# Pooled attention feeding an MLP: values of batch 0 pooled in halves, first h tiles by token halves, values of batch 1 loaded between the quarters of w2

## The chip, the cores and the metric

The kernel runs on one core of one Trainium2 chip. The metric is device time in microseconds; the number given for a kernel is the median of its runs. A profile is one separate execution with every instruction and DMA packet recorded.

A core has a matrix engine (PE, with a weight-load side PEld), VectorE (DVE), ScalarE (ACT), GpSimd (POOL) and SyncE (SP). PE writes PSUM, 8 banks of 512 fp32 columns on 128 partitions. DMAs are issued from SP, ACT or POOL; POOL's are the ones that convert types on the way.

## The reference

```python
# q, k, v: (8, 8, 576, 64) fp32; pool 8 -> 72 pooled rows per head
k_p = k.reshape(B, H, 72, 8, D).mean(axis=3)
v_p = v.reshape(B, H, 72, 8, D).mean(axis=3)
attn = softmax(q @ k_p^T / sqrt(D))
x = (attn @ v_p).transpose(0, 2, 1, 3).reshape(4608, 512)
h = x @ w_in            # 512 x 2048
g = h - tanh(h)
out = g @ w_out         # 2048 x 512
```

## The kernel before, in words

**Tiling.** A batch has 576 tokens. The first 512 of each batch make a token group (groups 0 to 7); the last 64 of all eight batches make group 8. For a group, h is computed transposed: 16 tiles of 128 features by 512 tokens, each from 4 matmuls over the 512 inputs (`w1b` stationary, `xT` moving), then Tanh on ACT and a subtraction on DVE into `Gt`. The second product uses `w2b`. Groups 1 to 8 do it with seven half-size products of sums of blocks of `Gt` and of w2 (L713 to L721): `w2s` holds the sums of w2 (`sum0` to `sum3`, `negated`), `w_sum` overwrites b12 in `w2b`, and DVE makes `P`, `Q`, `Dg` from `Gt`. Group 0 uses the plain product, `mlp_o(0, tb, qd, gts)` (L610): 4 token blocks by 4 quarters of w2 in the order `W2_ORDER = (0, 8, 4, 12)`.

**Order of the work.** The program has no scheduler (`manual_schedule`): each engine runs its instructions in the order in which the code issues them, so the code order is the order in each engine's queue, with semaphore waits between engines. A DMA issued from a queue whose semaphore is still held by an older DMA waits for that one; POOL has eight such semaphores and uses them in turn.

**Start (L783 to L1073).** Batch 0 and batch 1 are done by a special route so that PE has work while weights and inputs are still coming in. k of batch 0 is pooled on DVE (`pool_k`), turned on PE against an identity (`k_turn`), q is cast on ACT and turned on PE (`q_pe_transpose`), scores and exponentials follow (`scores_wide`). k and v rows lie as pairs of heads: 4 pairs of 128 rows, and 4 times 16 left-over rows in a fifth slot (`NM`). v of batch 0 is loaded by POOL as bf16 (`v_bf`) and pooled on PE: `v_pe_pool` accumulates 8 matmuls; `v_main` and `v_left` multiply with a mask into `VB`. `av_pair(p, half, b0)` computes attention times v for token blocks 2p and 2p+1 and four heads, normalises on DVE and writes `x0`; `x0_turn` turns it on PE and ACT copies it into `xT[0]`. `h_open` runs the first two of the four matmuls of h tiles 3, 0, 1, 2, 4. Between these steps stand `warm_pe(n)` calls (L777): matmuls on zeros that nothing reads. 30 are issued in all, 10 of them after q's last transposes.

Then tiles 0 to 4 get their other two matmuls and Tanh and subtraction (L975), tiles 5 to 15 follow (L980), and k, q, v of batch 1 and `mlp_o` of group 0 are interleaved (L1011 to L1069): `pool_k(1, nc.gpsimd, last=nc.vector)`, `k_transpose(1)`, `q_pe_transpose(1)`, `pool_v1` on DVE, `scores_wide(1)`, `av(1, blk)`, `turn1(blk)`.

**Loads that matter here.** POOL issues, in this order: v of batch 0 (L828), four quarters of w1 (`load_w1`), w2 rows 0 to 3 of 16 (`load_w2(0, 4)`), q of batch 1 (L838, L839), `load_w2(8, 4)`; after `pool_k(1)`, `load_w2(4, 4)` and `load_w2(12, 4)`. SP issues k of batch 1 when w1's second quarter has landed (L848), then v of batch 1 in two halves (L972, L973), and k of batch 2 when the third w2 load, `w2_dmas[2]`, has landed (L1043). ACT issues the left-over rows of v of batch 1 (L913); DVE pools them at L974.

**Groups 1 to 8 (L1075 to L1142).** `h_pair` makes two h tiles at a time, DVE subtracts (L646) and sums (L654); then the products, with scores and attention of the next batch among them. In group 1, DVE also runs `sum2(4)` (L1086) and the `w_sum` of b12 (L1088).

Of the kernel before, what the change touches and what calls it, by code (L numbers as in the profile page):

```python
# [20 lines left out]
R = 4  # L21
# [22 lines left out]
def kernel(  # L44
# [252 lines left out]
                out=vps[b][:, :, :], in0=r[:, :, 0, :], in1=r[:, :, 1, :], op=ALU.add  # L297
            )

    def pool_v1(ta, tb):  # L300
        r = v_raw[1].rearrange("p t (j d) -> p t j d", d=D)
        for n in (4, 2, 1):
            nc.vector.tensor_tensor(
                out=r[:, ta:tb, 0:n, :],
                in0=r[:, ta:tb, 0:n, :],
                in1=r[:, ta:tb, n : 2 * n, :],
                op=ALU.add,
            )
        if ta == NM:
            return v_left(VB[1], r[:, NM, 0:1, :], nc.vector)  # L310
        return v_main(VB[1], r[:, :, 0:1, :], nc.vector, ta, tb)

    vps = {}

# [6 lines left out]
    def v_main(vb, vs, eng, t0, t1):  # L321
        n = t1 - t0
        return eng.tensor_tensor(
            out=vb[:, 2 * t0 : 2 * t1, 0:D].rearrange("p (t s) d -> p t s d", s=2),
            in0=vs[:, t0:t1, :, :].to_broadcast([128, n, 2, D]),
            in1=mask[:, 2 * t0 : 2 * t1, :]
            .rearrange("p (t s) o -> p t s o", s=2)
            .to_broadcast([128, n, 2, D]),
            op=ALU.mult,
        )  # L330

    def v_left(vb, vs, eng):
        return eng.tensor_tensor(
            out=vb[:, 2 * NM :, 0:D],
            in0=vs.to_broadcast([128, NM, D]),
            in1=mask[:, 2 * NM :, :].to_broadcast([128, NM, D]),
            op=ALU.mult,
        )
# [67 lines left out]
    def scores_wide(b, ts):  # L406
        if b not in E_tiles:
            E_tiles[b] = work.tile([128, H, S], BF16, name="E", tag="E", bufs=1)[:, 0:NT, :]
        E = E_tiles[b]
        for t in ts:  # L410
            ps = ps_any([128, QA], FP32, "s_ps")
            score_mms(b, t, ps[:, :], False)
            nc.scalar.activation(out=E[:, t, 0:QA], in_=ps[:, :], func=ACT.Exp, scale=SCALE)
# [63 lines left out]
                stop=True,  # L477
            )

    def av_mms(b, blk, half, ps):  # L480
        E = E_tiles[b]
        vb = VB[b % 2]
        c0 = blk * 128 if blk < 4 else S - 128
        for n in range(3):
            t = 2 * half + n if n < 2 else NM
            s0 = 2 * t if n < 2 else 2 * NM + 2 * half
            nc.tensor.matmul(  # L487
                ps[:, 2 * n : 2 * n + 2, :].rearrange("p h d -> p (h d)")
                if n < 2
                else ps.rearrange("p (a s) d -> p a s d", s=2)[:, :, 1, :],  # L490
                lhsT=E[:, t, c0 : c0 + 128],
                rhs=vb[:, s0 : s0 + 2, :].rearrange("p h d -> p (h d)")
                if n < 2
                else vb[:, s0 : s0 + 2, :],
                start=(n == 0),
                stop=(n == 2),
                skip_group_check=True,
            )
# [82 lines left out]

    h_tiles = {}

    def mlp_h_mms(g, i, f0, f1, pool=None):
        if f0 == 0:
            h_tiles[i] = ps_h.tile([128, TG]) if pool is None else pool
        for fb in range(f0, f1):
            nc.tensor.matmul(
                h_tiles[i][:, :],
                lhsT=w1b[:, fb, i * 128 : (i + 1) * 128],  # L590
                rhs=xT[g][:, :, fb, :],
                start=(fb == 0),
                stop=(fb == NFB - 1),
            )

    def mlp_h_act(i, gts):
# [180 lines left out]
    def warm_pe(n, cols=512, b0=4):  # L777
        for _ in range(n):
            nc.tensor.matmul(
                bank(b0, [128, cols]), lhsT=zeros[:, 0:128], rhs=zeros[:, 0:cols], start=True, stop=True  # L780
            )
# [43 lines left out]
        )  # L825
    for i in range(2):
        nc.gpsimd.tensor_scalar_mul(VB[i][:, :, D:D1], mask[:, :, :], float(POOL))
    nc.gpsimd.dma_start(out=v_bf[:, 0:NM, :], in_=v_pairs[0, 0:128, :, :])  # L828
    nc.gpsimd.memset(spread[:, :], 0.0)
    nc.gpsimd.tensor_copy(  # L830
        out=spread.rearrange("p (t x) -> p t x", x=32)[:, :, 0:LO],
# [12 lines left out]
    nc.gpsimd.memset(k_raw[1][:, NM, :], 0.0)  # L844
    nc.gpsimd.memset(v_raw[0][:, NM, :], 0.0)
    nc.gpsimd.memset(KB[1][:, :], 0.0)

    after(load_k(1), w1_dmas[1])  # L848

# [50 lines left out]
    pool_k(0, nc.vector, NM, NT)  # L900
    warm_pe(2)
    q_pe_transpose(0, (2, 3), "act")
    warm_pe(2)
    scores_wide(0, (2, 3))
    k_turn_left()
    warm_pe(2)
    v_ps = v_pe_pool(NM, NT, spread)
    scores_wide(0, (NM,))
    v_left(VB[0], v_ps[:, 0, :, :], nc.vector)
    vs = v_pe_pool(0, NM, ident, 4)  # L910
    v_main(VB[0], vs, nc.vector, 0, 2)
    v_main(VB[0], vs, nc.vector, 2, 4)
    load_left(v_pairs, v_raw[1], 1, nc.scalar)  # L913
    gts = []

    def av_pair(p, half, b0):
        ps = PS[:, b0 : b0 + 2, 0 : 4 * D1].rearrange("p k (h d) -> p k h d", d=D1)
        for k in range(2):
            av_mms(0, 2 * p + k, half, ps[:, k, :, :])
        rden = work.tile([128, 2, 4, 1], FP32, name="rden2", tag="rden2")  # L920
        nc.vector.reciprocal(out=rden[:, :, :, :], in_=ps[:, :, :, D:D1])
        nc.vector.tensor_tensor(
            out=x0[:, 2 * p : 2 * p + 2, half, :, :],
            in0=ps[:, :, :, 0:D],
            in1=rden[:, :, :, :].to_broadcast([128, 2, 4, D]),
            op=ALU.mult,
        )
# [17 lines left out]
            in_=ps,  # L945
        )

    def h_open(i, b0):
        mlp_h_mms(0, i, 0, 2, bank(b0, [128, TG]))

    warm_pe(2, b0=3)
    av_pair(0, 0, 2)
    av_pair(1, 0, 5)
    av_pair(0, 1, 0)
    warm_pe(1)
    x0_turn((0, 1), 0, 7, nc.scalar.copy)
    av_pair(1, 1, 2)
    warm_pe(1)
    x0_turn((2, 3), 0, 5, nc.scalar.copy)
    warm_pe(2)  # L960
    h_open(3, 4)
    x0_turn((0, 1), 1, 7, nc.scalar.copy)
    h_open(0, 0)
    h_open(1, 1)
    x0_turn((2,), 1, 5, nc.scalar.copy)
    x0_turn((3,), 1, 6, nc.vector.tensor_copy)
    h_open(2, 2)
    h_open(4, 3)
    ps_any = ps_b1
    ps_h.n = ps_o.n = 0  # L970
    nc.scalar.copy(out=q_bf[:QT, R, :, :], in_=t0[:QT, :, R, :])
    load_main(v_pairs, v_raw[1], 1, 0, 2)  # L972
    load_main(v_pairs, v_raw[1], 1, 2, 4)  # L973
    pool_v1(NM, NT)  # L974
    for i in range(5):  # L975
        mlp_h_mms(0, i, 2, 4)
        mlp_h_act(i, gts)


    for i in range(5, NHID):  # L980
        mlp_h(0, i, gts, bank(i % 5, [128, TG]))
# [26 lines left out]
    def sum3(k0):  # L1008
        return w_sum(w2s[:, 3, :, :], b21, b11, ALU.subtract, k0=k0, k1=k0 + 4)

    pool_k(1, nc.gpsimd, last=nc.vector)  # L1011
    load_w2(4, 4)
    load_w2(12, 4)
    for h in (0, 4):
        nc.vector.tensor_copy(
            out=q_bf[:, 0:R, h : h + 4, :].rearrange("p j h d -> p h j d"),
# [9 lines left out]
    q_pe_transpose(1, (2, 3), "act")  # L1026
    q_pe_tail(1)
    scores_wide(1, (0,))
    pool_v1(2, 4)
    sum1(0)  # L1030
    mlp_o(0, 0, 1, gts)
    scores_wide(1, (1,))
# [4 lines left out]
    sum2(0)  # L1037
    sum0(0)
    sum3(0)
    mlp_o(0, 2, 1, gts)  # L1040
    mlp_o(0, 3, 1, gts)
    ps_a.n = 0
    after(load_k(2), w2_dmas[2])  # L1043
    load_v(2)
    load_q(2)
    av(1, 0, ps_any, True)
    av(1, 1, ps_any, True)
    sum1(4)
    sum0(4)
    mlp_o(0, 0, 2, gts)  # L1050
    turn1(0)
    mlp_o(0, 1, 2, gts)
    turn1(1)
    av(1, 2, ps_any, True)
    av(1, 3, ps_any, True)
    negated(1)
    sum3(4)
    mlp_o(0, 2, 2, gts)
    turn1(2)
    mlp_o(0, 3, 2, gts)  # L1060
    turn1(3)
    av(1, 4, ps_any, True)
    x_pairs.pop((1, 0))
# [1 line left out]
    x_dma_transpose(1, 2)  # L1065
    pool_k(2, nc.gpsimd)
    k_dma_transpose(2)
    for tb in range(4):
        mlp_o(0, tb, 3, gts)  # L1069
    load_k(3)  # L1070
    pool_v(2, nc.gpsimd, (0, 1))
    k_place(2, nc.gpsimd.tensor_copy)
# [2 lines left out]
    for g in range(1, NG):  # L1075
        nb = g + 1 if g + 1 < B else None
        nn = g + 2 if g + 2 < B else None
        for p in range(NP - 1):
            if g == 1 and 2 <= p < 5:
                q_cast_part(2, p - 2)  # L1080
                q_dma_transpose(2, p - 2)
            if nb is not None and g > 1 and p < 3:
                q_cast_part(nb, p)
            h_pair(g, p, ((6, 4, 2, 6, 0, 2, 4) if g == 1 else (0, 2, 4, 6, 0, 2, 4))[p], p % 2)
            if g == 1 and p == 1:
                sum2(4)  # L1086
            if g == 1 and p == 2:
                w_sum(b12, b22, b12, ALU.subtract)  # L1088
            if g == 1 and p == 4:
                store(0, 0, 2, nc.sync)  # L1090
                store(0, 2, 4, nc.sync)
                load_v(3)
                load_q(3)
                v_spread(2, nc.gpsimd)
            if 3 <= p < 6:
                sum_p(2 * p - 6, 2 * p - 4)
            if g > 1 and p == 0:
                if nb is not None:
                    k_dma_transpose(nb)
                store(g - 1, 2, 4, nc.gpsimd)  # L1100
                store(g - 1, 0, 2, nc.gpsimd)
                if nb is not None:
                    k_place(nb, nc.gpsimd.tensor_copy)
            if nb is not None and g > 1 and p < 3:
                q_dma_transpose(nb, p)
            if nb is not None and g > 1 and p == 2:
                v_spread(nb)
                if nn is not None:
                    load_k(nn)
                    load_v(nn)  # L1110
                    load_q(nn)
# [69 lines left out]
```

## Time and profile before

| | us |
|---|---|
| median of 3 runs | 285.9 (285.72 to 285.92) |
| profiled execution, own time | 286.52 |
| profiled execution, span of the core | 284.8 |
| PE busy (share of span) | 275.7 (97%) |
| DVE busy | 222.8 (78%) |
| ACT busy | 154.6 (54%) |
| POOL busy | 113.1 (40%) |
| group 1 h stage begins (L632) | 54.71 |
| group 2 h stage begins (L632, in the chain) | 84.32 |

The span is what the profile's times count from 0; the profiled execution took 1.7 us more than it. Durations are read from the profiled execution, and a change worked out from them is carried to the median. A matmul's recorded duration includes the time in the pipeline: 512 columns show 0.38 us, but they start 0.2155 us apart, and it is the distance that adds up. Idle time of PE is what counts when PE is the busiest engine; idle time of others is harmless unless PE waits for them.

In the timeline, a row is: start, busy time, engine, source line, operation, output<-inputs, shape, count, and in brackets the idle time of the engine before it with what ended it. "SPq", "ACTq" and the POOL rows named DMA_DIRECT2D are issues of DMAs, not their transfer. The trace also has, for each DMA, the times of its 16 completion signals, one from each DMA engine; a DMA has landed with the last of them.

### The profile page before, as it was taken

Reading aid. Unit: us, or ns where it says so; the run is one execution under the profiler, and the core shown is the slowest. Engines: PE = TensorE matmul, PEld = TensorE weight load, DVE = VectorE, ACT = ScalarE, POOL = GpSimd, SP = SyncE. Lnnn points to the kernel's source line nnn. Section 1 sums busy time; section 2 is a strip of 40 time slices with the busy share of each in tenths; the row PEclk is TensorE's granted clock in tenths of the full one; section 3 lists DMA queues with packets and bytes.
Section 4 is the critical chain, followed back from the end, with each engine's and each line's share of the span. In section 5 each row is a group of like instructions: output and inputs, shape, how many; then the busy total and the mean of one; then the engine's idle time right before and its main releaser. Section 6 shows DMA issues by size and latency. Waiting matters only on the chain.

```text
span 284.8 us, 5460 instructions
## 1 busy us (share of the span) xinstructions
PE 275.7 (97%) x2156; PEld 179.8 (63%) x2156; DVE 222.8 (78%) x342; ACT 154.6 (54%) x207; POOL 113.1 (40%) x125
## 2 busy tenths in 40 slices
PE   7799999999999999999999999999999999999994
PEld 2364445644894489548954895479547954884583
DVE  6569889489985998599859985998599839936983
ACT  4637656396528671857186708670868056216610
POOL 8630611991299019901990099009910110010000
PEclk9999999999999999999999999999999999999999
DMA  7999999999947894979789946896640540011014
GB/s 247 226 213 266 272 195 282 253 233 239 286 84 161 245 345 92 155 227 334 133 107 297 348 97 125 286 310 129 114 161 0 76 157 0 2 74 77 0 37 113
DMA packets 66731, 49.82 MB, mean 175 GB/s; under 512 B 42088, under 2 KB 55928, under 8 KB 66706
## 3 DMA queue, kind: packets, MB, share of 16 engines
q1 hardware_dynamic: 56082, 34.92, 48.9%
q0 software_dynamic: 8432, 12.72, 19.0%
q10 hardware_dynamic: 2192, 1.84, 2.2%
q8 instruction: 17, 0.28, 0.4%
q14 instruction: 8, 0.07, 0.1%
HBM read 36.70 MB, written 9.44 MB: 162 GB/s over the span
## 4 chain that ended last, share of the span: by engine, by line
PE 80%; DMA 12%; DVE 4%; POOL 1%; ACT 1%; issue 0%; ACTq 0%; POOLq 0%
PE PS L632 35%; PE PS L689 35%; DMA w2b<-in_moe_w_out_dram 9%; PE PS L616 4%; DMA v_raw<-in_v_dram 3%; PE PS L472 3%; PE PS L446 3%; DVE Gt L646 2%; DVE P L654 1%; PE PS L487 0%; PE PS L398 0%; DVE w2b L672 0%; ACT TS L645 0%; PE PS L566 0%; POOL w2s L839 0%
## 5 line engine op out<-in xcount | busy, mean ns | idle before, releaser
L632 PE MATMUL PS<-xT,w1b 128*128 128x512 bf16 (+1 forms) x504 | 98.0, 355 | 0.0
L646 DVE TENSOR_TENSOR Gt<-PS,TS 128x1024 bf16<-128x1024 f32 x56 | 68.3, 1220 | 35.3 <-ACT TS L645 35.3
L632 PEld LDWEIGHTS <-w1b 128*128 128x128 f16 x576 | 56.4, 98 | 52.8
L645 ACT ACTIVATE TS<-PS 128x1024 f32<-128x1024 f32 x56 | 57.4, 1025 | 29.6 <-PE PS L632 28.1
L733 POOL TENSOR_TENSOR m<-O,m 128x512 f32<-128x512 f32 x6 | 7.6, 1261 | 78.4 <-ACT m L731 78.4
L261 POOL TENSOR_TENSOR k_raw<-k_raw 128x512 f32<-128x512 f32 (+2 forms) x13 | 21.5, 1673 | 26.1 <-DMA k_raw<-in_k_dram 14.2
L689 PE MATMUL PS<-w2s,Dg 128*128 128x256 f16 x256 | 30.2, 272 | 0.0
L467 ACT ACTIVATE E<-PS 72x1024 bf16<-72x1024 f32 (+1 forms) x30 | 26.1, 930 | 4.2 <-PE PS L446 4.1
L689 PEld LDWEIGHTS <-Gt 128*128 128x128 bf16 x256 | 23.5, 98 | 6.8 <-issue 2.3
L689 PEld LDWEIGHTS <-P 128*128 128x128 bf16 x256 | 24.6, 98 | 3.0
L689 PEld LDWEIGHTS <-Dg 128*128 128x128 bf16 x256 | 24.6, 98 | 2.8
L654 DVE TENSOR_TENSOR P<-Gt 128x1024 bf16<-128x1024 bf16 x32 | 21.9, 686 | 0.5
L740 ACT COPY m<-PS 128x512 f32<-128x512 f32 x8 | 4.7, 586 | 29.6 <-PE PS L689 29.6
L664 DVE TENSOR_TENSOR Dg<-Gt 128x1024 bf16<-128x1024 bf16 x32 | 20.4, 681 | 0.0
L705 POOL DMA_DIRECT2D out_dram<-O x14 | 7.7, 553 | 31.6 <-DVE O L743 29.5
L523 DVE TENSOR_TENSOR x_sb<-PS,rden 128x512 bf16<-128x512 f32 x28 | 19.4, 691 | 1.0
L282 POOL TENSOR_TENSOR v_raw<-v_raw 128x512 f32<-128x512 f32 (+1 forms) x12 | 18.2, 1540 | 0.0
L689 PE MATMUL PS<-w2s,Gt 128*128 128x256 f16 x128 | 16.4, 273 | 0.0
L689 PE MATMUL PS<-w2b,P 128*128 128x256 f16 x128 | 16.3, 273 | 0.0
L689 PE MATMUL PS<-w2b,Gt 128*128 128x256 f16 x128 | 16.3, 272 | 0.0
L689 PE MATMUL PS<-w2s,Q 128*128 128x256 f16 x128 | 16.3, 272 | 0.0
L1143 ACT COPY O<-PS 128x512 f32<-128x512 f32 x7 | 4.1, 586 | 21.9 <-PE PS L689 21.9
(123 smaller groups left out, 394.9 us busy)
## 6 DMA issues: line engine op xcount, KB each, us to landing
k_raw<-in_k_dram SPq DMA_DIRECT2D x7, 1024.0 KB, 6.0
out_dram<-O POOLq DMA_DIRECT2D x14, 512.0 KB, 3.8
v_raw<-in_v_dram SPq DMA_DIRECT2D x6, 1024.0 KB, 8.1
q_raw<-in_q_dram SPq DMA_DIRECT2D x6, 1024.0 KB, 10.6
w1b<-in_moe_w_in_dram POOLq DMA_DIRECT2D x4, 512.0 KB, 14.9
w2b<-in_moe_w_out_dram POOLq DMA_DIRECT2D x4, 512.0 KB, 16.6
v_raw<-in_v_dram SPq DMA_DIRECT2D x2, 512.0 KB, 12.1
out_dram<-O SPq DMA_DIRECT2D x2, 512.0 KB, 4.2
```

The costliest lines, as they stand in the source:

```text
L261: eng.tensor_tensor(out=r[:, ta:tb, 0:4, :], in0=r[:, ta:tb, 0:4, :], in1=r[:, ta:tb, 4:8, :], op=ALU.add,)
L282: eng.tensor_tensor(out=r[:, ta:tb, 0:4, :], in0=r[:, ta:tb, 0:4, :], in1=r[:, ta:tb, 4:8, :], op=ALU.add,)
L446: nc.tensor.matmul(dst, lhsT=kv[a * D : (a + 1) * D, m, :], rhs=rhs, start=True, stop=True,)
L467: nc.scalar.activation(out=e, in_=ps, func=ACT.Exp, scale=SCALE)
L523: nc.vector.tensor_tensor(out=x_sb[:, :, :, :], in0=ps[:, :, :, 0:D], in1=rden[:, :, :, :].to_broadcast([128, 2, 4, D]), op=ALU.mult,)
L616: nc.tensor.matmul(o_ps[:, :], lhsT=gts[i][:, tb * 128 : (tb + 1) * 128], rhs=w2b[:, i, :], start=(i == 0), stop=(i == NHID - 1),)
L632: nc.tensor.matmul(dst[:, t0 * 128 : t1 * 128], lhsT=w1b[:, fb, i * 128 : (i + 1) * 128], rhs=x[:, t0:t1, fb, :], start=(fb == 0), stop=(f ...
L645: nc.scalar.activation(out=t2, in_=PS[:, b0 : b0 + 2, :], func=ACT.Tanh)
L646: nc.vector.tensor_sub(out=Gt[:, p, :, :], in0=PS[:, b0 : b0 + 2, :], in1=t2)
L654: nc.vector.tensor_tensor(out=P[:, a:b, :], in0=Gt[:, a:b, 0, :], in1=Gt[:, a:b, 1, :], op=ALU.add)
L664: return nc.vector.tensor_tensor(out=Dg[:, a:b, :, :], in0=Gt[:, a:b, :, 0:HT], in1=Gt[:, a:b, :, HT:TG], op=ALU.subtract,)
L689: nc.tensor.matmul(part(g, bk, tt), lhsT=lhs(k, slice(tt * 128, (tt + 1) * 128)), rhs=rhs[:, k, :], start=(first and k == 0 and (tt == 0 o ...
```

## The change

What it does, part by part:

1. v of batch 0 is loaded by two DMAs of two head pairs each, and pooled on PE in two halves: pairs 0 and 1 ahead of `scores_wide(0, (2, 3))`, pairs 2 and 3 after the left-over scores. The left-over part is pooled ahead of `k_turn_left`.
2. `av_pair(·, 0, ·)` is split: the matmuls of pairs 0 and 1 for both block pairs, then those of the left-over rows, then the normalisation. The h tiles 0 to 3 are built in quarters by `h_part`: two of the four matmuls, for two of the four token blocks, with 256 columns each. Tile 4 is made whole afterwards. PSUM banks are assigned anew. Six of the 30 `warm_pe` matmuls go.
3. The left-over rows of v of batch 1 are pooled on POOL at L914's place instead of on DVE after the h openings.
4. The two main loads of v of batch 1 are issued by POOL: the first between `load_w2(8, 4)` and `load_w2(4, 4)`, the second between `load_w2(4, 4)` and `load_w2(12, 4)`. The two w2 loads are issued before `pool_k(1)` instead of after it. k of batch 2 waits for the second v load instead of `w2_dmas[2]`.
5. `pool_v1(2, 4)` on DVE comes after the sums; `mlp_o` of w2's third quarter for blocks 0 and 1 comes ahead of `av(1, 0)`, and the later `mlp_o` calls move up by two places each.
6. `sum2(4)` and the `w_sum` of b12 move from inside group 1 to ahead of it.

```diff
-    def pool_v1(ta, tb):
+    def pool_v1(ta, tb, eng=nc.vector):
...
+    def mlp_h_mms(g, i, f0, f1, pool=None, t0=0, t1=4):
+                h_tiles[i][:, t0 * 128 : t1 * 128],
+                rhs=xT[g][:, t0:t1, fb, :],
+                start=(fb == 0 and t0 == 0),
...
-    nc.gpsimd.dma_start(out=v_bf[:, 0:NM, :], in_=v_pairs[0, 0:128, :, :])
+    for ta in (0, 2):
+        nc.gpsimd.dma_start(out=v_bf[:, ta : ta + 2, :], in_=v_pairs[0, 0:128, ta : ta + 2, :])
...
+    load_main(v_pairs, v_raw[1], 1, 0, 2, nc.gpsimd)
+    load_w2(4, 4)
...
-    warm_pe(2)
+    vs0 = v_pe_pool(0, 2, ident, 4)
+    v_main(VB[0], vs0, nc.vector, 0, 2)
+    warm_pe(1, b0=3)
     scores_wide(0, (2, 3))
+    v_ps = v_pe_pool(NM, NT, spread)
     k_turn_left()
-    warm_pe(2)
-    v_ps = v_pe_pool(NM, NT, spread)
+    v_left(VB[0], v_ps[:, 0, :, :], nc.vector)
+    warm_pe(1, b0=3)
     scores_wide(0, (NM,))
-    v_left(VB[0], v_ps[:, 0, :, :], nc.vector)
-    vs = v_pe_pool(0, NM, ident, 4)
-    v_main(VB[0], vs, nc.vector, 0, 2)
-    v_main(VB[0], vs, nc.vector, 2, 4)
+    vs1 = v_pe_pool(2, 4, ident, 3)
+    v_main(VB[0], vs1, nc.vector, 2, 4)
     load_left(v_pairs, v_raw[1], 1, nc.scalar)
+    pool_v1(NM, NT, nc.gpsimd)
+    v1_last = load_main(v_pairs, v_raw[1], 1, 2, 4, nc.gpsimd)
+    load_w2(12, 4)
...
+    def h_part(i, half, tp, b0=None):
+        pool = None if half or tp else bank(b0, [128, TG])
+        mlp_h_mms(0, i, 2 * half, 2 * half + 2, pool, 2 * tp, 2 * tp + 2)
+
+    av_pair(0, 0, 1, (0, 1))
+    av_pair(1, 0, 6, (0, 1))
+    av_pair(0, 0, 1, (2,))
+    av_pair(1, 0, 6, (2,))
+    av_pair(0, 1, 3)
+    warm_pe(1, b0=5)
+    x0_turn((0, 1), 0, 0, nc.scalar.copy)
+    av_pair(1, 1, 1)
+    warm_pe(1, b0=5)
+    x0_turn((2, 3), 0, 0, nc.scalar.copy)
+    for i, b0 in ((0, 6), (1, 7), (2, 5)):
+        h_part(i, 0, 0, b0)
+    x0_turn((0, 1), 1, 4, nc.scalar.copy)
+    h_part(3, 0, 0, 3)
+    for i in range(3):
+        h_part(i, 0, 1)
+    x0_turn((2, 3), 1, 0, nc.scalar.copy)
+    nc.scalar.copy(out=q_bf[:QT, R, :, :], in_=t0[:QT, :, R, :])
+    h_part(3, 0, 1)
+    for i in range(4):
+        h_part(i, 1, 0)
...
-    load_main(v_pairs, v_raw[1], 1, 0, 2)
-    load_main(v_pairs, v_raw[1], 1, 2, 4)
-    pool_v1(NM, NT)
-    for i in range(5):
-        mlp_h_mms(0, i, 2, 4)
+    for i in range(4):
+        h_part(i, 1, 1)
         mlp_h_act(i, gts)
+    mlp_h(0, 4, gts, bank(4, [128, TG]))
...
     pool_k(1, nc.gpsimd, last=nc.vector)
-    load_w2(4, 4)
-    load_w2(12, 4)
...
-    pool_v1(2, 4)
     sum1(0)
...
     sum3(0)
+    pool_v1(2, 4)
     mlp_o(0, 2, 1, gts)
     mlp_o(0, 3, 1, gts)
+    mlp_o(0, 0, 2, gts)
+    mlp_o(0, 1, 2, gts)
     ps_a.n = 0
-    after(load_k(2), w2_dmas[2])
+    after(load_k(2), v1_last)
...
-    for tb in range(4):
-        mlp_o(0, tb, 3, gts)
+    mlp_o(0, 2, 3, gts)
+    mlp_o(0, 3, 3, gts)
+    sum2(4)
+    w_sum(b12, b22, b12, ALU.subtract)
...
-            if g == 1 and p == 1:
-                sum2(4)
-            if g == 1 and p == 2:
-                w_sum(b12, b22, b12, ALU.subtract)
```

## The prediction

> **What bounds the kernel now.** I read the page first: PE is busy 97% of the span and every slice of its clock row is 9, so at the right clock only PE's filler and gaps can be won. Then the chain of waits in order of time (start, length, what), to see what PE waits for before its steady groups:
>
> ```profile
> 13.75 26.33 DMA w2b<-in_moe_w_out_dram
> ...
> 40.12 1.02 PE PS L616 x4
> ...
> 60.71 0.81 DVE w2s L672
> 61.52 1.13 DVE Gt L646
> 62.66 1.18 DVE w2b L672
> ...
> 69.16 1.15 DVE Gt L646
> ...
> 70.35 0.41 PE PS L446 x2
> ```
>
> The second quarter of w2 lands at 40.1 and PE starts on it that moment; later VectorE, with two weight sums (L672) among the Gt subtractions, releases PE at 70.35. Third, the timeline from 0 to 70 us (start, busy, engine, line, what, idle before and its releaser):
>
> ```profile
> 15.02 0.59 PE L779 MATMUL PS<-xT_last 128*128 128x512 bf16 x2
> ...
> 17.23 0.40 PE L934 MATMUL PS<-ident,P 128*128 128x128 bf16 x4
> ...
> 18.30 0.59 PE L779 MATMUL PS<-xT_last 128*128 128x512 bf16 x2
> ...
> 19.14 0.59 PE L588 MATMUL PS<-xT,w1b 128*128 128x512 bf16 x2 [0.24 <-ACT xT L941]
> ...
> 21.94 1.01 DVE L303 TENSOR_TENSOR v_raw<-v_raw 128x256 f32<-128x256 f32 x3 [0.43 <-DMA v_raw<-in_v_dram]
> ...
> 30.90 2.90 POOL L261 TENSOR_TENSOR k_raw<-k_raw 128x1280 f32<-128x1280 f32 x1 [14.21 <-DMA k_raw<-in_k_dram]
> ...
> 35.91 0.81 DVE L270 TENSOR_TENSOR kd<-k_raw 128x640 bf16<-128x640 f32 x1
> ...
> 37.19 0.76 DVE L1015 COPY q_bf<-w2s 128x1024 bf16<-128x1024 bf16 x2 [0.46 <-DMA w2s<-in_q_dram]
> ```
>
> Filler (L779) stands between the attention steps of batch 0; the first h matmul runs at 19.14. POOL idles 14.2 us until k of batch 1 lands. Last, busy time by stretch (length, then PE, PEld, DVE, ACT, POOL, clock, DMA share, GB/s):
>
> ```profile
> 34.47:40.12 5.65, 5.29 (x43) 2.94 (x42) 4.90 (x11) 2.38 (x5) 2.42 (x3) 1.00 1.29 198
> 68.54:84.32 15.78, 15.35 (x171) 12.92 (x170) 14.91 (x25) 7.07 (x10) 7.44 (x5) 1.00 0.79 196
> 98.15:113.14 14.99, 14.99 (x171) 12.66 (x169) 13.98 (x24) 6.59 (x9) 7.38 (x5) 1.00 0.84 247
> ```
>
> The products of group 1 take 15.78 against 14.99 in group 2: 0.79 us are lost to VectorE.
>
> **What the Trainium skill says.** (1) "DMA: Bandwidth & Descriptors", Issuing engines are not separate DMA queues: loads from SP, ACT and POOL share the same 16 engines. The trace agrees: DMA share is over 1.2 from 23 to 40 us, so moving v from SP to POOL changes order, not volume. (2) The same page, Latency and other measured facts: two of the 16 engines are usually slower on POOL's queue. Agrees: of the 16 completions of w2's second quarter fourteen came by 38.66, the last two at 39.83 and 40.08. I therefore reckon by last completions. (3) "TensorE: Matmul & The Clock Gate", Part 1: the clock falls back after an idle window of about 3.4 us. Here 1.5 us of idle before 10.68 cost nothing (512 columns still 0.2155 us apart), so dropping filler is safe. (4) "PSUM — Partial Sum Buffer", The four PSUM rules: a starting matmul clears the accumulate bits of its whole bank; so one start per h tile serves both token halves, at no extra instruction.
>
> **The change part by part.** PE times are starts in the narrow timeline.
>
> *Batch 0, h by halves.* Both kernels end q's transposes at 11.82. Pooling v's first half (8 x 0.056 = 0.45) now comes there; it needs the first of two v loads. Before, v's packets were written by 11.7, and completions came from 11.87 to 13.47 (slow engine). Half as many packets: bounds 11.2 and 13.5, I take 11.9. Scores 2 and 3 wait for ACT's copy at 12.73 anyway, the left-over scores for VectorE's copy at 13.73: 13.80, as now. Then v's second half 14.13 to 14.58, and the (0,1) parts of AV (8 x 0.058) at 14.58 instead of 15.70. The NM parts need the exponential that ends at 14.85: 15.05. VectorE's first normalisation (0.2 + 0.7) ends at 16.28 instead of 17.18, so the first x turn is at 16.33 instead of 17.23. The second must wait for ACT's copy out of the same bank 0: 17.42. Then h starts on two blocks at 17.66 (19.14 now): 6 half matmuls, turn 3 (VectorE 17.94: no wait) at 18.31, and all the rest without a wait: 20 x 0.2155 + 2 x 0.23 from 17.66 gives 22.43 for the start of tile 5, against 24.06. **Lead 1.63.** Six of 30 fillers go (1.29), the rest is idle time. Halving costs nothing: 256 columns take 0.109 in the L689 rows. w1 is there: quarters land at 16.6, 19.8, 22.4, 26.3, needed at 17.7, 21.6, 25.2, 29.2.
>
> *Left rows of v1 to POOL.* VectorE drops 1.47 us, unneeded there. On POOL 448 elements plus a 256-element product at 2.42 ns (L267: 1.55 us for 640) make 1.8 (bounds 1.4, VectorE's price, and 2.6). It starts when the rows land at 21.7 and sits in POOL's 14.2 us of idle. Queued behind it on POOL: the issues of v1's second half and w2's last quarter, which wait for older loads of the same semaphores (22.4, 26.3), then pool_k(1), which waits until 30.9 anyway.
>
> *Where the lead stops.* Products with w2's first quarter would end at 35.43 (37.06 now). k of batch 1 is tied to w1's second quarter as now and shares the engines as now: it lands at 30.7, POOL ends at 35.42, VectorE's kd (0.81, no longer behind a subtraction) at 36.3. k's turn starts at 36.37: **lead 0.69**, 0.94 given back.
>
> *v1 between w2's quarters.* Its 1 MB leaves SP's ring, where it ran from 29 to 34 beside POOL's queue. At 340 GB/s (SP's rate at 46 to 50) that is 3.0 us, by which POOL's queue moves up: q1 lands at 34.1 (37.16), w2's second quarter at 37.1 (40.08). q's cast now follows kd: gap 0.07 instead of 0.33; the wait of 0.35 before 40.12 goes. PE starts that quarter at 38.85: **lead 1.27**. Then v1's first half, w2's third quarter (2.55, spacing of such loads now), second half, last quarter. An f32 load on POOL's queue isn't shown: bounds 1.45 (SP's rate) and 2.55 (a cast load); I take 1.5. Landings: 38.5, 41.0, 42.5, 45.3 (the last 45.78 now). pool_v1(0,2) waits on VectorE until 38.5; behind it are only weight sums, nothing PE needs. Four sums (2.49) end at 43.0, pool_v1(2,4) (1.9) at 44.95. PE reaches av(1,0) at 38.85 + 4.68 (as from 40.12 to 44.80) + 8 x 0.2155 = 45.26: **no wait, 0.3 spare.** Both moved mlp_o pairs only swap places; the quarters they need are there by 43.5 and 49.2. SP's k2 load is released at 42.6 as now (42.65). Group 1 starts at 53.45 instead of 54.71.
>
> *The two weight sums ahead of group 1.* 0.9 + 1.25 of VectorE move into its idle 3.9 us before 57.77 (the second waits for the last mlp_o at 53.7, ends 54.9, first subtraction 56.4). The last pair's subtraction then ends about 0.7 earlier against PE, just when PE wants that bank: 0.75 of the 0.79 is won. What is late next: nothing; groups 2 to 8 are PE's.
>
> Sum: 1.26 + 0.75 = 2.0. Span 284.8 to 282.8; the profiled run's own time 286.52 (1.72 outside the span) to 284.5. The median, 285.9, stood 0.6 under that run, and becomes **283.9**.
>
> **Rivals.** *v1 a little late*: its loads cost 2.55 each, v1's second half lands at 44.4, is pooled at 46.35, and PE idles 1.1 before av(1,0): 285.0; half of it 284.5. For: POOL's queue ran at 200 GB/s alone. Against: that is the rate of casts. *The weights' queue doesn't move up* (q1 and w2 land as now; something else limits it): only the group-1 gain stays, 285.15. Against: the DMA share over 1.2 is work that leaves. *The early v half lands late* (13.5): the lead at tile 5 falls to 0.3, total 1.65, 284.25; it belongs to my case's range. *Slower, one mechanism*: v1, now behind 512 KB of w2 in one queue, takes nothing of the freed share and is paid at 2.55 behind an unchanged 40.08: second half 47.7, pooled 49.7. PE stands at av(1,0) for 4.4 us: 288.3. It decides from the point where v1's second half lands after 45.3 (pooled 47.3; 45.26 + 2.0), 2.8 us beyond my estimate.
>
> **How the numbers follow.** My case 0.57, from 283.0 (k lands 0.3 earlier, no wait anywhere) to 284.4. v1 a little late 0.20, 284.4 to 285.2. Queue not moved up 0.10, 285.0 to 285.6. Slower 0.13, 286.5 to 288.3. A measurement tells about 0.2%, 0.6 us, from no change. Faster: 0.57 + 0.20 and 0.04 of the third case, 0.81; same 0.06; slower 0.13. Range 283.0 to 285.4.
>
> **What would show it.** Right: h tile 5 at 22.4, k's turn released by kd near 36.4, no DMA wait before w2's second quarter, L323 ended before av(1,0) near 45.3, group 1 at 53.5, its products in 15.0. Wrong: a gap before the AV matmuls of batch 1 released by VectorE (v late), or a gap before the k turn longer than 1 us (k late), or group 1's products still at 15.8.

## The result and the profile after

The time did not change. The changed kernel takes 285.75 us (285.37 to 288.63, 12 runs), the kernel before 285.8 in the same session (12 runs): ratio 1.0007 with a 95% interval of 0.9983 to 1.0031. The profiled execution of the changed kernel took 285.73, its span is 283.9, so this profile stands for the median. The first profile of the kernel before did not (286.52). The kernel before was therefore profiled again; that execution took 285.46 with a span of 283.7, and is the one compared with here, called *before, second profile*. It lies 0.3 under the median, as the first lay 0.7 over it, so leads of 0.3 read against it are not to be pressed.

The medians in this document are of all runs; the ratios leave out the five runs that took over 1.5% more than the fastest run of their kernel, and follow the means, so the two can differ.

**Where PE gets ahead.** The rows of the changed kernel's timeline that answer to those of before:

```profile
16.75 0.82 PE L588 MATMUL PS<-xT,w1b 128*128 128x256 bf16 x6
...
29.13 2.90 POOL L261 TENSOR_TENSOR k_raw<-k_raw 128x1280 f32<-128x1280 f32 x1 [1.62 <-DMA k_raw<-in_k_dram]
...
33.68 0.82 DVE L270 TENSOR_TENSOR kd<-k_raw 128x640 bf16<-128x640 f32 x1 [0.15 <-POOL k_raw L267]
...
34.60 0.44 PE L352 MATMUL PS<-ident,kd 128*128 128x128 bf16 x5
...
37.11 1.02 PE L617 MATMUL PS<-w2b,Gt 128*128 128x512 f16 x4
...
38.70 1.48 DVE L303 TENSOR_TENSOR v_raw<-v_raw 128x512 f32<-128x512 f32 x3 [2.61 <-DMA v_raw<-in_v_dram]
...
42.97 1.47 DVE L303 TENSOR_TENSOR v_raw<-v_raw 128x512 f32<-128x512 f32 x3
...
43.51 0.34 PE L487 MATMUL PS<-VB,E 128*128 128x130 bf16 x3
...
44.47 0.43 DVE L323 TENSOR_TENSOR VB<-v_raw,mask 128x256 bf16<-128x256 f32 x1
...
44.95 0.68 PE L487 MATMUL PS<-VB,E 128*128 128x130 bf16 x9 [1.10 <-DVE VB L323]
```

The first h matmul, the k turn and w2's second quarter (L617) start at 16.75, 34.60 and 37.11. In the second profile of before they stand at 18.25, 36.36 and 39.34, the last as its chain of waits has it, right behind the load of that quarter:

```profile
39.34 1.02 PE PS L616 x4
```

PE's wait of 0.3 for that load is gone, as foreseen. But PE is at attention times v by 43.51, does three of twelve matmuls, and stops until VectorE has pooled v's second half.

**Where it loses the lead.** PE's waits from 8 to 90 us (who waited, for what, total, times, longest):

```profile
PE PS L487 <- DVE VB L323: 1.1, 1, 1.1
PE PS L633 <- DVE Gt L647: 0.6, 1, 0.6
PE PS L633 <- DMA xT<-x_sb: 0.5, 1, 0.5
...
```

Measured as the distance between matmul starts beyond the normal one, these are 1.26, 0.73 and 0.66 us. None of the three is in either profile of before. The chain of waits of the changed kernel (start, length, what) shows the work behind them:

```profile
15.87 22.81 DMA v_raw<-in_v_dram
40.65 2.40 DVE w2s L673 x4
...
53.96 1.53 DVE w2s L673
55.49 2.21 DVE w2b L673
57.70 1.15 DVE Gt L647
58.89 8.79 PE PS L633 x40
...
79.13 4.86 DMA xT<-x_sb
84.03 13.12 PE PS L633 x64
```

Its first piece is v's *first* half, landed at 38.68. Behind it VectorE is busy without a break: pooling that half (1.95), four weight sums (2.49), pooling the second half (1.93), to 44.90. The second half, landed at 42.33, waits 0.64 behind the sums. Next come the two moved sums, and last a DMA transpose of x for group 2, which took 4.86 us.

The stretches that held the stall in the products of group 1, in the changed kernel (length, then PE, PEld, DVE, ACT, POOL, clock, DMA share, GB/s):

```profile
67.52:82.50 14.98, 14.98 (x169) 12.66 (x168) 13.98 (x24) 6.59 (x9) 7.26 (x5) 1.00 0.92 231
82.50:84.03 1.53, 1.04 (x10) 0.78 (x8) 0.44 (x1) 1.32 (x2) 1.53 (x2) 1.00 0.24 42
```

The products take 14.98 without a gap: that stall is gone. Right behind them PE idles for the transposes.

The whole account, starts in us:

| | before, second profile | after | lead of after | what happened |
|---|---|---|---|---|
| first h matmul | 18.25 | 16.75 | 1.50 | batch 0 shortened |
| k turn | 36.36 | 34.60 | 1.76 | k lands 0.3 earlier too |
| w2's second quarter | 39.34 | 37.11 | 2.23 | no DMA wait |
| group 1, h | 53.93 | 52.96 | 0.97 | 1.26 lost waiting for v |
| group 1, products | 67.76 | 67.52 | 0.24 | 0.73 lost behind the sums |
| group 2, h | 83.25 | 82.50 | 0.75 | the products' stall (0.49) won |
| group 3, h | 112.07 | 111.98 | 0.09 | 0.66 lost for the x transposes |

2.23 + 0.49 is won, 1.26 + 0.73 + 0.66 given back: 0.07 is left. The end of the kernel takes that too: the last products start at 267.20 against 267.29, and the spans are 283.9 against 283.7.

### The profile page after: what moved, and what is told of

It is laid out like the page before. It is cut to its first block, busy times and chain, and to the rows that moved or that the text cites. A ratio compares the mean times of both kernels' runs of the same rounds, so it can differ in the third digit from the quotient of the medians.

```text
span 283.9 us, 5492 instructions
## 1 busy us (share of the span) xinstructions
PE 274.5 (97%) x2174; PEld 180.9 (64%) x2174; DVE 224.2 (79%) x337; ACT 154.8 (55%) x207; POOL 118.5 (42%) x132
## 4 chain that ended last, share of the span: by engine, by line
PE 75%; DMA 12%; DVE 9%; POOL 2%; issue 1%; SPq 0%; DVEq 0%
PE PS L633 37%; PE PS L690 33%; DMA v_raw<-in_v_dram 8%; PE PS L446 3%; PE PS L472 2%; DVE w2s L673 2%; DMA k_raw<-in_k_dram 2%; DMA xT<-x_sb 2%; DVE x_sb L523 2%; DVE v_raw L303 1%; DVE w2b L673 1%; DVE rden L522 0%; DVE O L626 0%; DVE Gt L647 0%; POOL w2s L841 0%
## 5 line engine op out<-in xcount | busy, mean ns | idle before, releaser
L282 POOL TENSOR_TENSOR v_raw<-v_raw 128x512 f32<-128x512 f32 (+1 forms) x12 | 19.6, 1656 | 0.0
```

The costliest lines, as they stand in the source:

```text
L282: eng.tensor_tensor(out=r[:, ta:tb, 0:4, :], in0=r[:, ta:tb, 0:4, :], in1=r[:, ta:tb, 4:8, :], op=ALU.add,)
```

## Two causes in the trace

**VectorE behind GpSimd.** The timeline of the changed kernel around the sums:

```profile
47.08 1.28 DVE L673 TENSOR_TENSOR w2s<-w2b 128x1024 f16<-128x1024 f16 x2
...
49.96 1.96 DVE L673 TENSOR_TENSOR w2s<-w2b 128x1024 f16<-128x1024 f16 x1
...
53.41 1.53 POOL L270 TENSOR_TENSOR kd<-k_raw 128x640 bf16<-128x640 f32 x1
53.88 1.61 DVE L673 TENSOR_TENSOR w2s<-w2b 128x1024 f16<-128x1024 f16 x1
...
54.90 4.47 POOL L282 TENSOR_TENSOR v_raw<-v_raw 128x512 f32<-128x512 f32 x2
...
55.42 2.29 DVE L673 TENSOR_TENSOR w2b<-w2b 128x2048 f16<-128x2048 f16 x1
...
57.62 3.59 DVE L647 TENSOR_TENSOR Gt<-PS,TS 128x1024 bf16<-128x1024 f32 x3
...
58.89 3.40 PE L633 MATMUL PS<-xT,w1b 128*128 128x512 bf16 x15 [0.57 <-DVE Gt L647]
```

With GpSimd idle, a `w2s` sum takes 0.68 (the two at 47.08 take 1.28 together, overlapping a little). Here the one at 53.88 ends at 55.49, 0.54 after GpSimd's operation (53.41 to 54.95) has ended; the one at 55.42 ends at 57.70, 1.08 after GpSimd's next has (56.62). GpSimd's operation after that, the second of the two in the L282 row, starts at 56.58 and takes 2.80 where it takes 1.81 in the second profile of before: it ends 1.68 after VectorE has. Each looks as if it waited for the other's instruction to end and then ran at its own pace. It is not peculiar to the change: in the second profile of before a `w2s` sum also meets GpSimd's sum (48.79 to 50.59) and ends 0.55 after it:

```profile
49.20 1.94 DVE L672 TENSOR_TENSOR w2s<-w2b 128x1024 f16<-128x1024 f16 x1
```

The Trainium skill, "GPSIMD Engine Reference", section 1 (Specifications), says that GpSimd shares its SBUF interfaces with VectorE and that there is contention with VectorE instructions of two SBUF inputs. The trace agrees as to which instructions suffer, and shows how much: up to nearly a whole instruction of the other engine. Subtractions from PSUM (`Gt<-PS,TS`) keep their 1.2 us.

**PE's instruction fetch.** The trace has a DMA queue named "instruction" with 17 packets of 16 KB in the whole span. That is one for some 256 matmuls or weight loads of PE on average, so they are taken here for fetches of PE's instructions; the trace doesn't name the engine that they serve. Each packet lasts 0.9 to 1.4 us, the two that matter below 0.97 and 0.89. The change adds 18 matmuls with 18 weight loads net (4326 to 4362 rows), so every fetch comes at another place in the program: the second at 33.83 (41.76 before), while q, w2 and v are loading, and the fifth at 81.72 (84.03 before), while the x transposes of group 2 are under way. A DMA is complete only with the last of its 16 engines, so one engine that a fetch keeps busy could hold all of it up. That is a theory until the fetches are moved.

## The experiments

None leaves out or changes part of the computation. Each ratio is against the kernel before, run beside it.

| run | what | median | ratio, 95% interval |
|---|---|---|---|
| e0 | kernel before, profiled run | 285.46 | |
| e1 | changed, both sums back | 285.77 | 1.0008 (0.9996 to 1.0019) |
| e2 | changed, old head | 284.93 | 0.9994 (0.9971 to 1.0017) |
| e3 | changed, two stores on POOL | 287.3 | 1.0043 (1.0026 to 1.0059) |
| e4 | changed, 15 fillers out | 285.12 | 0.9973 (0.9963 to 0.9983) |
| e5 | e2, 36 PE rows more | 285.71 | 0.9997 (0.9989 to 1.0005) |
| e6 | changed, one sum back | 285.68 | 1.0004 (0.9991 to 1.0016) |
| e7 | e2, one sum back | 285.54 | 0.9991 (0.9976 to 1.0007) |
| e8 | changed, 28 PE rows fewer | 284.6 | 0.9968 (0.9955 to 0.998) |
| e9 | changed, one output block ahead of av | 284.92 | 0.9974 (0.9962 to 0.9986) |
| e10 | e8, one sum back | 284.52 | 0.9961 (0.9949 to 0.9972) |
| e11 | e8, e9 and e10 together | 285.33 | 0.9983 (0.9966 to 0.9999) |

### The kernel before again, and one part undone at a time

e0 is the kernel before, unchanged:

> The kernel before, unchanged, profiled a second time. Its first profile ran 0.6 us over its median. Theory of walls (the lead of the change is given back at three waits: v of batch 1, the weight sums beside POOL, the x transposes behind SP's loads): here k of batch 0 lands about 1 us earlier than in the first profile (its last main piece near 8.0 us instead of 9.0), the h stage of group 2 starts near 83.5 instead of 84.3, span about 284.0. Rival (the first profile was typical of the kernel before): same positions as in it within 0.3 us, span 284.8.

It gave the second profile of before. Its k of batch 1 landed at 29.29, where the first had 30.73, and PE's wait for k of batch 0 at 9 us was 0.53 instead of 1.63. So about 0.8 of the first profile's lateness at group 1 (54.71 against 53.93) was that execution's own. Group 2 starts at 83.25, as expected.

e1 puts both sums back:

```diff
     mlp_o(0, 3, 3, gts)
-    sum2(4)
-    w_sum(b12, b22, b12, ALU.subtract)
...
+            if g == 1 and p == 1:
+                sum2(4)
+            if g == 1 and p == 2:
+                w_sum(b12, b22, b12, ALU.subtract)
```

> The changed kernel with the two weight sums back inside group 1 (sixth part undone). Theory of walls: the PE gap of about 0.95 us before the fourth h pair of group 1 is gone, the products of group 1 lose about 0.8 us again, so 285.5 to 286.1 us, no change within 0.2%. Rival (my sum: that part is worth 0.75 us): 286.4 to 286.6.

285.77. The wait at 58 is gone, and PE waits 0.68 in the products instead, as it did before. Part 6 is worth nothing: it moves the loss from behind the pairs to in front of them.

e2 takes parts 1 and 2 back, and keeps the rest:

```diff
-    av_pair(0, 0, 1, (0, 1))
-    av_pair(1, 0, 6, (0, 1))
...
-    for i, b0 in ((0, 6), (1, 7), (2, 5)):
-        h_part(i, 0, 0, b0)
+    av_pair(0, 0, 2)
+    av_pair(1, 0, 5)
...
+    h_open(3, 4)
+    x0_turn((0, 1), 1, 7, nc.scalar.copy)
+    h_open(0, 0)
```

> The changed kernel with the first two parts undone (v of batch 0 by one load, h opened over all 512 tokens, all 30 fillers); loads, POOL's left rows and the weight sums as changed. Theory of walls: h tile 5 starts 1.6 us later, but the wait for v of batch 1 before its attention shrinks by what is lost, and the later waits too: 285.5 to 286.2. Rival (the head's lead reaches the end): 286.5 to 287.3.

Both expectations missed: 284.93, 0.8 under the changed kernel by the medians. Its interval against before does not exclude 1: four of its 18 runs lie at 287.67 to 288.18, and nothing on record says why. In its profile h starts 1.30 later than in the changed kernel (18.05) and the k turn 1.18 later (35.78), yet group 1 starts at 52.74, not later than the changed kernel's 52.96: there is no wait for v, and none for the x transposes. So the 1.3 us that the new head wins are worth nothing behind v; and the transposes, which are issued at the same time in both (79.06, 79.13), land at 82.16 in one and at 83.99 in the other. What differs there is the number of PE rows: the old head has 36 fewer.

e3 tested a remedy of another theory, that stores from SP hold up the loads behind the transposes:

```diff
-                store(0, 0, 2, nc.sync)
-                store(0, 2, 4, nc.sync)
...
+                store(0, 0, 2, nc.gpsimd)
+                store(0, 2, 4, nc.gpsimd)
```

> The changed kernel with the two stores of group 0 issued by POOL after v's spread instead of by SP ahead of the loads of v and q of batch 3. Theory of walls: those loads start 1.1 us earlier and have SP's ring to themselves, the transposes of x of batch 2 land in 3 us instead of 4.9, the wait of 0.76 us at the start of group 2 is gone: 285.0 to 285.3. Rival (the transposes take their time for another reason): 285.75, the wait stays.

It is slower, 287.3: the loads of batch 3 land as before, but the second store lands at 75.55 (70.85 in the changed kernel), and PE waits 2.07 at 74.32 for an output tile that is not yet stored. The transposes still take 3.70, and PE waits 0.77 for them. That theory is dropped.

### Moving the fetches

e5 is the cleanest test: the kernel of e2 with six of its fillers of 512 columns cut into 24 of 128. PE's columns and all work behind it are the same; only 36 rows are added.

```diff
-    warm_pe(9)
+    warm_pe(3)
+    warm_pe(24, cols=128)
```

> The old head with the new tail (284.9 so far), with six of its first nine fillers cut into 24 of 128 columns: the same PE time and 36 PE rows more, as many as the new head adds. Fetch theory: the second fetch comes at 34 to 36 us, the fifth near 82; the x transposes of batch 2 take 4 to 5 us instead of 3.1 and PE waits for them, v1's second half may be late too: 285.5 to 285.8. Rival (the new head costs by its own order): 284.9, no wait for the transposes.

285.71, as the fetch theory said; 0.8 above e2 by the medians. The fifth fetch came at 81.41. The start of group 2 in the timeline, e2 first, then e5:

```profile
82.43 7.74 PE L633 MATMUL PS<-xT,w1b 128*128 128x256 bf16 x43
```

```profile
82.02 1.04 PE L633 MATMUL PS<-xT,w1b 128*128 128x256 bf16 x8
83.55 6.65 PE L633 MATMUL PS<-xT,w1b 128*128 128x256 bf16 x34 [0.49 <-DMA xT<-x_sb]
```

With thirty-six rows more of filler near the start, PE waits 75 us later. The wait for v did not come with them (the old head has no lead to lose).

How much of the time this is worth is less clear. The profiled execution of e5, 285.06, is the lowest of its 13 runs and only 0.14 above that of e2: it reaches group 2 0.41 earlier, loses 0.65 there, and is 0.25 behind at group 3 (111.50 against 111.25). By the ratios the two kernels don't differ, because of e2's four runs near 288. What makes a typical run of e5 0.8 slower is not in a profile.

e5 settles something else. It has as many PE rows as the changed kernel, 4362, and the old head: 285.71 against 285.75. At equal rows the new head is worth nothing in the end.

e8 goes the other way: the changed kernel with 28 rows fewer, the early fillers and the rest of the order kept.

```diff
-    for i in range(4):
-        h_part(i, 1, 0)
     ps_any = ps_b1
     ps_h.n = ps_o.n = 0
     for i in range(4):
-        h_part(i, 1, 1)
+        mlp_h_mms(0, i, 2, 4)
         mlp_h_act(i, gts)
```

and six `warm_pe` fillers behind the k turn out.

> The changed kernel with 28 PE rows fewer: the second half of the inputs of h tiles 0 to 3 in full matmuls again (8 fewer) and six late fillers dropped (the early ones, which bring the clock up, stay). Order and data are the same. Fetch theory: the second fetch of PE's instructions moves from 33.8 to about 35.5, the fifth from 81.7 to about 82.5, behind the x transposes of batch 2, which land in 3.1 us; PE's wait of 0.66 for them goes, the waits for v (1.26) and for the sums (0.73) stay within 0.4: 285.1. Rival (the new order makes the transposes late): the wait stays, 285.75.

284.6: 1.15 under the changed kernel, more than expected. The fifth fetch came behind the landing of the transposes and PE's wait for them is gone. So are, in its profile, the other two waits (that profile is the lowest of its 22 runs, 283.77). Its waits from 20 to 95 us:

```profile
PE PS L588 <- ACT xT L948: 0.5, 1, 0.5
PE PS L487 <- ACT xT L573: 0.2, 1, 0.2
```

The first is new: full matmuls on the second inputs need the last x turn 0.6 sooner. PE starts tile 5 at 22.26 against 21.55, and nothing is lost by that later. So e8 changes PE's times as well as its rows, and its gain can't be put down to the fetch alone.

e4 drops all fillers but the first nine (30 rows):

```diff
-    warm_pe(1)
...
-    warm_pe(2)
...
-    warm_pe(6)
```

and six more like them.

> The changed kernel without its 15 filler matmuls of 512 columns behind the first nine: 30 PE rows fewer, so that the fetches of PE's instructions (one DMA packet of 16 KB for every 256 PE instructions) come almost where they came in the kernel before. Fetch theory: the second fetch comes near 40 us and not near 33.8, the fifth near 84 and not near 81.7; v1's second half has all its completions by about 41.3 (42.33 in the changed kernel), the wait for VB before attention times v falls from 1.26 to 0.2 to 0.5 us, the x transposes of batch 2 land in about 3.1 us instead of 4.9 and PE's wait of 0.66 for them goes: about 284.7. Rival (the head's own order, not the fetches, makes v and the transposes late): both waits stay, 285.5 to 285.9. If the fillers are what keeps the clock up: a lower clock before 20 us and more than 286.5.

285.12. No wait for v nor for the transposes, but it is no clean test of v: h starts at 18.29, 1.5 later, so PE also comes later to v. There the trace shows the third case of the expectation, a lower clock before 20 us (though not the time over 286.5 that went with it). In the row of the granted clock, 40 slices of which 9 is full, it is the second slice:

```profile
PEclk9599999999999999999999999999999999999998
```

The clock was at half from 8.43 to 15.26, though PE's longest idle time up to 9.5 us was 1.35. No other kernel here has such a stretch before its last 3 us. That e4 is faster all the same says again that the head's lead is not what sets the time.

Over all kernels the fifth fetch sorts the transposes without an exception:

```
run   transpose issued   fetch after issue   transpose took   PE waits
e3    82.62              0.49                3.70             0.77
e6    78.58              2.58                5.13             0.93
after 79.13              2.59                4.86             0.66
e9    78.34              2.71                4.86             0.65
e1    79.03              2.73                4.90             0.70
e5    78.65              2.76                4.86             0.65
e4    79.15              3.06                3.11             -
e11   80.25              3.10                3.07             -
e10   78.44              3.23                3.10             -
e0    79.88              4.15                3.04             -
e7    78.68              4.29                3.09             -
e2    79.06              4.97                3.10             -
```

(e8's were issued at 77.80, landed at 81.12, ahead of its fetch at 81.47; in the first profile of before the fetch came 4.07 behind the issue and the transpose took 3.05.) Where a fetch came less than 2.8 us behind the issue, the transpose took 0.6 to 2.0 us longer than the usual 3.1; in the others the fetch came when the transpose was over or within 0.05 of it.

The 16 completions tell more. In e1, e5 and e9, where the fetch came 2.71 to 2.76 behind the issue, fifteen are about on time and one is late: in e5 fifteen come by 81.87 and the last at 83.51. That is what one engine held up would look like. But in the changed kernel all sixteen are late, from 83.75 to 83.99, and so they are in e6 and e3; and the delay there, 1.8 and 2.0 in the first two, is longer than the packet, 0.9 to 1.0. So how the fetch acts on the transpose stays open. For v the sorting is weaker: v's first half landed at 37.69 to 38.68 (mean 38.34) in the six kernels whose second fetch comes at 33.8 to 34.3, and at 37.06 to 38.18 (mean 37.44) in the six of the new tail whose second fetch comes at 38.7 to 40.9. The two overlap: the fetch may be a part of v's lateness, not the shown whole of it. In the changed kernel the last of 16 completions was already 0.95 behind the one ahead of it in the load of q (32.44 and 33.39), before the fetch at 33.83.

### The sums, and all together

e6 is the changed kernel with only `sum2(4)` ahead of group 1:

```diff
     sum2(4)
-    w_sum(b12, b22, b12, ALU.subtract)
...
+            if g == 1 and p == 2:
+                w_sum(b12, b22, b12, ALU.subtract)
```

> The changed kernel with only one of its two late weight sums (sum2 of the second half) ahead of group 1; the sum into b12 goes back behind the third pair of group 1. My theory (a VectorE sum of two SBUF operands that meets a running GpSimd sum waits for its end, so that the two sums together end at 57.7 instead of 56.4): the first Gt subtraction is free of them, PE's gap of 0.73 at 58 goes, and one sum among the pairs costs at most 0.3 in the products: 285.1. Rival (the time lost there is made up or lost again at the x transposes or in the products whatever the order): 285.7.

285.68: the rival's number. In its profile (285.3, 0.4 under the median) the gap at 58 is gone, but 0.49 came back in the products and the wait for the transposes grew to 0.93. e7 is the same edit on e2:

> The old head with the new tail (284.9 so far), with the same split of the two sums as in the run before. My theory: the gap of 0.87 at 58 goes, at most 0.3 comes back in the products of group 1: 284.2. Rival: 284.9, the time is lost again in the products of group 1 or behind them.

285.54, where neither had it. The profiled run took 284.49 with no wait at 58 and one of 0.73 in the products, put down to `qT<-q_bf`, a transpose. Its 22 runs fall into groups, 284.2 to 285.0 (7 runs), 285.4 to 285.9 (10 runs) and 287.1 to 288.9 (5 runs); only the first has a profile, so what makes the others is open.

e9 changes only the order of PE's own work in the changed kernel:

```diff
     mlp_o(0, 1, 2, gts)
+    mlp_o(0, 2, 2, gts)
     ps_a.n = 0
...
-    mlp_o(0, 2, 2, gts)
-    turn1(0)
     mlp_o(0, 3, 2, gts)
+    turn1(0)
+    mlp_o(0, 0, 3, gts)
     turn1(1)
```

and so on, each later call one place up.

> The changed kernel with one more token block of the group 0 output product (0.87 us of PE) ahead of attention times v of batch 1, taken from behind the last such product, so that v has 0.87 us more. Theory of the walls (each later wait is set by VectorE, GpSimd and transfers that don't move with PE): the wait for v falls from 1.26 to about 0.4, but the one for the sums grows from 0.73 to about 1.4 or the one for the transposes to 1.5: 285.6 to 285.9. Rival (the waits add up, each its own loss): 284.9.

284.92. My theory that the next wait would take up what this one gave is refuted, and the rival's number came. Its profile (284.99) has no wait for v and none at 58 (PE's one for the transposes, 0.65, stays). But it doesn't show that the waits simply add up. In that execution PE was 0.85 behind from the start (first h at 17.60), VectorE had pooled v by 44.34 instead of 44.90, and group 1 starts only 0.15 earlier than in the changed kernel. Most of the gain is the gap at 58: there the first of the two sums started just ahead of GpSimd's operation (53.58 and 53.70), took 0.68, and both were done at 56.74 instead of 57.70.

e10 puts e8 and e6 together:

> The changed kernel with the 28 rows fewer and with the second of its two late weight sums back behind the third pair of group 1. Theory of the walls: no wait at 58 and none for the transposes; the wait for v (1.26) stays, the products of group 1 lose up to 0.5: 284.5. Rival (one of the two remedies is worth nothing in the other's company): 285.1.

284.52, as expected; 1.23 under the changed kernel. Its profile, 284.42, is typical for it, and shows what is left:

```profile
PE PS L446 <- DVE Gt L647: 0.3, 1, 0.3
PE PS L487 <- DVE VB L323: 0.3, 1, 0.3
...
```

By matmul starts 0.51, 0.45, and 0.62 in the head, 1.58 in all; the changed kernel has 1.26 + 0.73 + 0.66 = 2.65. The difference, 1.07, accounts for most of the 1.23.

e11 adds e9's order to that:

> All three remedies in the changed kernel: 28 rows fewer, the second sum back among the pairs, one more output block ahead of attention times v. Theory of the walls: the wait for v is about 0.4, none at 58, none for the transposes, the products of group 1 lose up to 0.5: what the change gave back in three places falls to 0.9, so 283.9. Rival (a fourth wait, of VectorE or of the loads of k and v of batch 3, stands just behind): 284.5 or more.

285.33, as bad as the rival said. Its profile shows a wait that neither named:

```profile
51.23 0.40 PE L566 MATMUL PS<-ident,x_sb 128*128 128x128 bf16 x4 [1.20 <-DVE x_sb L523]
```

With one product fewer behind it the x turn waits for a normalisation on VectorE, 1.36 us by matmul starts, and that one stands behind two weight sums which took 2.36 instead of 1.28, beside a sum of GpSimd. But this profile (286.24) lies 0.9 over the median: seven of the 14 runs are at 284.4 to 284.9, like most of e10's, and have no profile. e10 (5 runs) and e8 (22 runs) are the best versions here and can't be told apart.

## Why the prediction was wrong

**Batch 0, h by halves: right in kind, worth nothing.** Tile 5 starts at 21.55, where 22.43 was foreseen, because k of batch 0 came earlier; against the second profile of before (23.36) the lead is 1.81. But e2 and e4 give 1.3 to 1.5 of it up and are no slower, and e5 equals the changed kernel at the same number of PE rows. Dropping six fillers was safe, as said: the clock stays at full. As a rule it isn't, and no idle window of 3.4 us is needed: in e4, with 15 more gone, the clock fell to half and h came 1.5 later, with no idle time of PE over 1.35 before. That one start per h tile serves both token halves is built into the changed kernel; no run varies it.

**Left rows of v1 to POOL: right.** POOL's sums and product take 1.66 and 0.62 there, 2.3 in all (1.8 foreseen, bounds 1.4 and 2.6), in idle time.

**Where the lead stops: failed.** k was taken to land at 30.7, "as now", from the one profile at hand, where it was late; it landed at 28.99 (29.29 in the second profile of before). The k turn came at 34.60, not 36.37. PE's way from there to `av(1, 0)` was foreseen as 8.89 and took 8.91, so PE stood there at 43.51 instead of 45.26.

**v1 between w2's quarters: the loads right, "no wait, 0.3 spare" failed.** The loads landed within 0.5 of the estimates (38.68, 41.00, 42.33, 44.79), and VectorE was done at 44.90 (44.95 foreseen). The rival *v1 a little late* named this place, but for another reason: v was on time and PE early. (Its own sum is a little short: three loads at 2.55 behind 37.1 end at 44.75, not 44.4. And the DMA share, said to be over 1.2 from 23 to 40, was 1.14 from 23 to 26.) v is what sets the start of group 1, so the gain against a typical run is 0.97 there, not 1.26. The first profile was itself 0.8 late at that point, by its own k; I took all of the 1.26 for the change, and the 0.6 between its time and the median off besides.

**The two weight sums: failed in size.** 0.9 + 1.25 was reckoned; they took 1.61 + 2.29, and the first subtraction came at 57.62, not 56.4. Their prices were those of sums that meet no GpSimd work. They cost 0.73 in front and brought 0.49 behind, where + 0.75 was foreseen. The 0.79 behind that figure was read too high: 84.32 is the start of group 2 in the chain, but its first matmul stands at 84.15, so that the first profile's stall was 0.62. e1 confirms the sum of nothing.

**"What is late next: nothing": failed.** The x transposes of group 2 were: 0.66. The halved matmuls were costed at nothing because the columns add up; their rows in the instruction stream (36 with all else) were not counted. That these rows bring the wait is what e5, e4 and e8 bear out; how they do it is open.

The sum: foreseen 2.0; 0.29 less at v, 0.26 less in the products, 0.73 at the sums and 0.66 at the transposes make 1.94, which leaves the 0.07 of the account. The slower rival (v behind w2 at 2.55 a load) did not occur: the two v loads followed the w2 loads ahead of them by 1.62 and 1.32.

## What to carry over

Before a lead is counted, find the next work that does not move with it (here the pooling of v on VectorE), and take the starts of before from a profile whose time is near the median. Price an operation by a row that has the same neighbours on the engine beside it: the sums cost 1.8 times their row once GpSimd ran. And count PE instructions, not only columns: 36 more (e5) and 28 fewer (e8) went with 0.8 and 1.15 us of the median, of which the profiles show 0.65 as a wait for one transpose.

## What the hardware showed unexpectedly

- The queue named "instruction" carried 17 packets of 16 KB, one for some 256 PE rows, of 0.9 to 1.4 us in the changed kernel. 36 filler rows at the start (e2 to e5) brought one into a transpose 75 us later: 4.86 us instead of 3.10, and a wait of 0.65 for PE. That it holds up one DMA engine fits the completions of three kernels and not those of the changed one; the order in time is shown in all.
- VectorE sums with two SBUF inputs and GpSimd's sums look as if they took turns by nearly whole instructions: 0.68 became 1.61 and 1.96 on VectorE, 1.81 became 2.80 on GpSimd.
- Dropping fillers can halve the clock without any long idle time. With 15 out (e4) it was at half from 8.43 to 15.26, PE's longest idle time up to 9.5 us being 1.35; with only six later ones out (e8, e10) it stayed at full. The mean of e4's profile, 0.985, hides this, and so does the total: nothing was lost in the end.
